# State products of two groups moved into the core visits before them, and one group cut into blocks of 64 tokens

## The chip, the core and the metric

The kernel runs on one core of a Trainium2 chip. The metric is the device time of one execution in microseconds. Before the change the median was 227.49 us over three runs (227.48 to 227.77). The kernel before was run again beside every experiment, on the same chip. A run more than 1.5% above the fastest of the same kernel counts as slow, and slow runs enter no comparison here.

The engines are written as in the profile: PE is TensorE (PEld its weight loads), DVE is VectorE, ACT is ScalarE, POOL is GpSimd and SP is SyncE. SP computes nothing here. It issues nearly all the loads, one after the other, so I call it the load queue. ACT issues the writes of the results.

## What must be computed

Linear attention with a decay per head comes first, then a SwiGLU feed-forward block (FFN) on its result. Cut to what matters:

```python
# q, k, v: (4 batches, 8 heads, 768 tokens, 64); lam: one decay per head
for each block of tokens:
    intra = (q k^T * mask of powers of lam) v       # scores, mask, product with v
    inter = (q * powers of lam) kv_state            # what came before the block
    out   = intra + inter
    kv_state = lam^block * kv_state + (k * powers of lam)^T v      # "state products"
x   = out as (3072, 512)
res = (silu(x @ w_gate) * (x @ w_val)) @ w_out      # 512 -> 1536 -> 512
```

The reference takes blocks of 64 tokens. A kernel is free to take others, as long as the decays are right.

## The kernel before

The work comes in 12 groups of 256 tokens. Two groups make a tile of 512 tokens, on which the FFN runs in 12 chunks of 128 columns. A chunk is four gate and four value products. A "step" is a chunk on a whole tile, and a "half step" is a chunk on one of its groups. The attention of a later group is dropped in between the steps of an earlier tile. TensorE then leaves its 128x128 FFN products for a burst of 64x64 products, and I call such a burst a visit.

A group below `NAT0` is taken in two blocks of 128 tokens. From `NAT0` on it is taken in four blocks of 64. This also decides how it is loaded:

```python
    NAT0 = 6
# ... cut ...
    def load_fp32(g, eng, src, what, h0=0, h1=H):
        # ... cut: the tile ...
        if g < NAT0:
            eng.dma_start(out=t[:, h0:h1], in_=gsrc(src, g, h0)[:, 0:h1 - h0])
            return
        # ... cut ...
        parts = [(0, 128, False)] if what == "v" else [(0, M, False), (M, M, True)]
        for s in range(2):
            for p0, n, rev in parts:
                eng.dma_start(out=t[p0:p0 + n, :, s * D:s * D + D], in_=...)
```

So a group in two blocks takes three loads (k, q, v). A group in four blocks takes ten (four for k, four for q, two for v), for the same bytes.

A group passes through these functions. `cast_scaled` makes bf16 of k (ACT) and q (DVE) and issues a transpose by DMA on the load queue. `v_scale` scales v on GpSimd. `scores` are the q k products, and their masks run on DVE. `upd_mm`, `upd_copy` and `state` are the state products on TensorE, their copies by ACT and the adding up on GpSimd. The core is the rest:

```python
    def guard(g):        # one column, copied by ACT: intra waits for it
        t = const.tile([128, 1], FP32, name="guard", tag="guard", bufs=2)
        nc.scalar.copy(out=t, in_=st[("op", g)][1][:, 511:512])
# ... cut ...
    def core_a(g):
        st[("op", g)] = [bank() for _ in range(2)]
        inter(g, True)
        guard(g)

    def core_b(g, fns=(nc.scalar.copy, nc.scalar.copy)):
        run_later(len(later))
        intra(g, False)
        evac(g, fns)
# ... cut ...
    def ahead(g):        # upd = upd_mm, upd_copy, state
        upd(g)
        scores(g)
```

A plan says after which step what comes. `s1a` and `s1b` are the half steps of tile 1 on its first and second group, and `s2` is the last of the first half steps of tile 2. The part concerned:

```python
    at(s1a[3], cast_scaled, 4)
    at(s1a[3], load_group, 5)
    for c in range(0, FC, 2):
        at(s1a[3], wo_piece, c, c + 2)
    # ... cut: scores and state products of 3 ...
    at(s1a[9], core_a, 3)
    at(s1a[10], core_b, 3, SPLIT)
    # ... cut ...
    at(s1b[3], cast_scaled, 5)
    at(s1b[3], load_group, 6)
    at(s1b[4], wo_cast)
    at(s1b[4], wo_cast)
    at(s1b[6], ahead, 4)
    # ... cut: three wo_cast, v_scale 5 ...
    at(s1b[9], core_a, 4)
    at(s1b[10], core_b, 4, SPLIT)
    at(s1b[10], wo_cast, ACTC)
    NH = 4
    s2 = [step(2, fc, 0, 2) for fc in range(NH)][-1]
    at(s2, load_group, 7, "kq")
    at(s2, ffn_out, 0, 0)
    at(s2, ahead, 5)
    at(s2, run_later, 3)
    at(s2, ffn_out, 0, 1)
    at(s2, core_a, 5)
    at(s2, ffn_out, 0, 2)
    at(s2, core_b, 5)
    at(s2, cast_scaled, 6)
    at(s2, load_group, 7, "v")
    at(s2, v_scale, 6, nc.gpsimd)
    at(s2, ffn_out, 0, 3)
```

`wo_piece` loads a sixth of w_out and `wo_cast` makes bf16 of it. `ffn_out(0, b)` is the output product of tile 0 (12 products over w_out), its copy by ACT and its write, issued by ACT. The order of the plan is also the order in which each engine meets its own instructions: nothing overtakes.

## Time and profile before

| | before |
|---|---|
| time, median of 3 | 227.49 us |
| span in the profile, mean clock | 226.7 us, 1.000 |
| busy: PE, DVE, ACT, POOL | 96%, 40%, 47%, 40% |
| first scores of 3 to the inter products of 6 | 48.44 to 99.67 us |

TensorE is the bound. This is the queue's own timeline before the change (start, duration, queue and source line, the kind of DMA, output and input, how many in a row):

```profile
49.03 1.18 SPq L100 DMA_DIRECT2D kraw<-in_k_dram  x1
50.25 0.93 SPq L100 DMA_DIRECT2D qraw<-in_q_dram  x1
51.22 1.03 SPq L100 DMA_DIRECT2D v<-in_v_dram  x1
...
78.28 3.08 SPq L107 DMA_DIRECT2D qraw<-in_q_dram  x4
83.43 2.01 SPq L256 DMA_TRANSPOSE qkt<-qk  x1
```

The first three lines are the loads of group 5, issued within 3.22 us. The fourth is q of group 7, issued in four pieces. The last is the transpose of group 6, whose scores TensorE reaches at about 91 us. It is issued some 8 us ahead.

### The profile page before, as it was taken

What the parts mean: (1) busy time and instruction counts of PE and PEld (TensorE: products, weight loads), DVE (VectorE), ACT (ScalarE), POOL (GpSimd) and SP (SyncE); (2) the same over time, 40 slices, a digit from 0 to 9 for tenths busy, and PEclk for the clock granted to TensorE, in tenths of its full rate; (3) what the DMA queues carried; (4) which work ended last, traced back from release to release, by engine and by line L of the source; (5) the groups of instructions that cost most, each with busy time, mean ns of one, the idle gap of its engine ahead of it and who ended that gap; (6) DMA issues with size and microseconds to landing.
All of it is one profiled execution on the core that took longest, in us unless ns stands there. A gap on an engine that the chain in (4) does not pass through costs nothing.

```text
span 226.7 us, 6032 instructions
## 1 busy us (share of the span) xinstructions
PE 218.6 (96%) x2492; PEld 121.5 (54%) x2504; DVE 91.0 (40%) x156; ACT 107.2 (47%) x212; POOL 90.1 (40%) x133
## 2 busy tenths in 40 slices
PE   8889979999999999999999999999999999999994
PEld 4565445887876465454544544544544444444442
DVE  2663446586763602733434362253242123222200
ACT  5878556655653263455454463453433433322321
POOL 6675636833492720968563092092160000000000
PEclk9999999999999999999999999999999999999999
DMA  6999999999998989197688848908101101101122
GB/s 200 344 345 328 371 314 326 260 174 343 402 208 195 230 214 264 46 236 186 164 185 220 210 109 210 247 8 142 49 1 46 49 0 46 46 3 46 46 93 93
DMA packets 88028, 39.70 MB, mean 175 GB/s; under 512 B 57666, under 2 KB 83522, under 8 KB 88002
## 3 DMA queue, kind: packets, MB, share of 16 engines
q1 hardware_dynamic: 83490, 32.58, 56.4%
q10 hardware_dynamic: 4512, 6.75, 8.3%
q8 instruction: 19, 0.31, 0.6%
q14 instruction: 7, 0.06, 0.1%
HBM read 28.31 MB, written 6.29 MB: 153 GB/s over the span
## 4 chain that ended last, share of the span: by engine, by line
PE 84%; DMA 7%; SPq 5%; POOL 2%; issue 1%; ACT 0%; DVE 0%; DVEq 0%
PE bank L552 27%; PE bank L519 25%; PE bank L534 24%; DMA qraw<-in_q_dram 4%; SPq L100 3%; DMA wraw<-in_moe_w_val_dram 3%; SPq L218 2%; PE bank L479 2%; PE bank L466 2%; PE bank L387 1%; PE bank L331 1%; PE bank L357 1%; PE bank L294 1%; POOL wv_sb L665 1%; POOL kvf L426 0%
## 5 line engine op out<-in xcount | busy, mean ns | idle before, releaser
L537 DVE TENSOR_TENSOR h<-sil,bank 128x512 bf16<-128x512 bf16 (+1 forms) x91 | 51.9, 576 | 108.3 <-PE bank L534 85.0
L519 PE MATMUL bank<-xt,wg_sb 128*128 128x512 bf16 (+1 forms) x364 | 77.2, 335 | 0.0
L534 PE MATMUL bank<-xt,wv_sb 128*128 128x512 bf16 (+1 forms) x364 | 77.0, 335 | 0.0
L523 ACT ACTIVATE sil<-bank 128x512 bf16<-128x512 f32 (+1 forms) x91 | 46.2, 511 | 43.2 <-PE bank L519 38.3
L552 PE MATMUL bank<-wo_sb,h 128*128 128x512 bf16 (+2 forms) x288 | 64.2, 370 | 0.8 <-issue 0.3
L534 PEld LDWEIGHTS <-wv_sb 128*128 128x128 bf16 x364 | 35.5, 98 | 27.0 <-POOL wv_sb L665 0.4
L519 PEld LDWEIGHTS <-wg_sb 128*128 128x128 bf16 x364 | 33.9, 98 | 26.3 <-DVE xt L491 0.5
L552 PEld LDWEIGHTS <-h 128*128 128x128 bf16 x300 | 28.6, 98 | 32.5
L554 ACT COPY osb<-bank 128x512 f32<-128x512 f32 (+1 forms) x24 | 14.0, 582 | 55.4 <-PE bank L552 55.4
L243 POOL TENSOR_TENSOR v_s<-v,dec 128x1024 bf16<-128x1024 f32 (+1 forms) x15 | 23.4, 1568 | 20.8 <-DMA v<-in_v_dram 10.8
L426 POOL TENSOR_TENSOR kvf<-kvs,ups 128x256 f32<-128x256 f32 x8 | 5.8, 728 | 34.6 <-ACT ups L409 32.0
L338 DVE TENSOR_TENSOR ssb<-bank,causal 128x512 bf16<-128x512 f32 x24 | 15.3, 684 | 4.5 <-PE bank L331 4.4
L491 ACT CAST xt<-bank 128x512 bf16<-128x512 f32 x20 | 12.2, 660 | 2.9 <-PE bank L479 2.4
L435 POOL CAST kvn<-kvf 64x256 bf16<-64x256 f32 x24 | 12.5, 520 | 1.5
L426 POOL TENSOR_TENSOR kvf<-kvf,ups 128x256 f32<-128x256 f32 x16 | 11.6, 726 | 0.6
L409 ACT COPY ups<-bank 128x256 f32<-128x256 f32 (+1 forms) x24 | 9.5, 449 | 2.4 <-PE bank L387 1.4
L263 ACT CAST qk<-kraw 128x1024 bf16<-128x1024 f32 x9 | 9.4, 1042 | 0.4 <-DMA kraw<-in_k_dram 0.4
L265 DVE TENSOR_TENSOR qk<-qraw,qdn 128x1024 bf16<-128x1024 f32 x6 | 8.2, 1372 | 2.6 <-DMA qraw<-in_q_dram 2.6
L362 DVE TENSOR_TENSOR ssb<-bank,causaln 128x512 bf16<-128x512 f32 x12 | 8.3, 688 | 1.2 <-PE bank L357 1.1
L237 POOL CAST wo_sb<-woraw 128x1024 bf16<-128x1024 f32 x5 | 5.1, 1042 | 6.3 <-DMA woraw<-in_moe_w_out_dram 6.3
L479 PE MATMUL bank<-ssb,v_s 64*64 64x128 bf16 (+1 forms) x384 | 6.7, 207 | 0.5 <-ACT guard L450 0.5
L479 PEld LDWEIGHTS <-v_s 64*64 64x64 bf16 x384 | 5.3, 105 | 2.0 <-issue 2.0
(66 smaller groups left out, 121.5 us busy)
## 6 DMA issues: line engine op xcount, KB each, us to landing
out_dram<-osb ACTq DMA_DIRECT2D x23, 256.0 KB, 2.9
v<-in_v_dram SPq DMA_DIRECT2D x18, 256.0 KB, 4.5
woraw<-in_moe_w_out_dram SPq DMA_DIRECT2D x6, 512.0 KB, 7.7
kraw<-in_k_dram SPq DMA_DIRECT2D x24, 128.0 KB, 3.8
qraw<-in_q_dram SPq DMA_DIRECT2D x24, 128.0 KB, 3.8
wraw<-in_moe_w_gate_dram SPq DMA_DIRECT2D x5, 512.0 KB, 7.5
wraw<-in_moe_w_val_dram SPq DMA_DIRECT2D x5, 512.0 KB, 6.5
kraw<-in_k_dram SPq DMA_DIRECT2D x4, 512.0 KB, 6.2
```

What stands on the lines that cost most here:

```text
L243: eng.tensor_tensor(out=st[("vs", g)][:, h0:h1], in0=st[("v", g)][:, h0:h1].rearrange("p h (s d) -> p h s d", s=2), in1=vfac(g, h0, h1), o ...
L338: nc.vector.tensor_tensor(out=ssb[:, h2, 2 * c:2 * c + 2].rearrange("p a s n -> p a (s n)"), in0=sp[(c, h2)].rearrange("p (a x) -> p a x", ...
L426: nc.gpsimd.tensor_tensor(out=o, in0=f, in1=u, op=ALU.add)
L435: nc.gpsimd.tensor_copy(out=o[64 - h2 * 64:128 - h2 * 64], in_=f[h2 * 64:h2 * 64 + 64])
L479: nc.tensor.matmul(op[r][h2 * 64:h2 * 64 + 64, cols(g, hp, s)], v_s[ps, 2 * hp + h2, s], ssb[ps, h2, hp * 2 + s] if g >= NAT0 else ssb[ps, ...
L491: fns[r](out=xt[:, g % 2, :, r].rearrange("p h (m s) -> p h s m", s=2) if g < NAT0 else xt[:, g % 2, :, :, r * M:r * M + M], in_=op[r].rea ...
L519: nc.tensor.matmul(gp[:, 0:N], wg_sb[:, mc, fs], xt[:, b0 // 2:b1 // 2, mc].rearrange("p g b n -> p g (b n)"), start=(mc == 0), stop=(mc = ...
L523: nc.scalar.activation(sil[:, 0:N], gp[:, 0:N], AF.Silu)
L534: nc.tensor.matmul(vp[:, 0:N], wv_sb[:, mc, fs], xt[:, b0 // 2:b1 // 2, mc].rearrange("p g b n -> p g (b n)"), start=(mc == 0), stop=(mc = ...
L537: nc.vector.tensor_tensor(out=h_sb[:, fc % FH, b0:b1].rearrange("p b n -> p (b n)"), in0=sil[:, 0:N], in1=vp[:, 0:N], op=ALU.mult)
L552: nc.tensor.matmul(ps, st[("h", t, fc // FH)][:, fc % FH, b], wo_sb[:, fc, c0:c1], start=(fc == 0), stop=(fc == FC - 1))
L554: fn(out=osb[:, c0:c1], in_=ps)
```

## The change

The intent has three parts. The state products of groups 4 and 5 move into the core visits of groups 3 and 4, between the inter and the intra products, where TensorE waits for the guard copy anyway. Group 5 becomes a group in four blocks of 64 tokens, which makes its scores, inter and intra products narrower. The order around it is fitted to this: one more half step before the first outputs, the cast of group 5 two half steps later, the last two pieces of w_out behind it, and the w_out casts spread over three engines.

```diff
-    NAT0 = 6
+    NAT0 = 5
@@
+    def core_upd(g, fns):
+        run_later(len(later))
+        core_a(g)
+        upd_mm(g + 1)
+        core_b(g, fns)
+        upd_copy(g + 1)
@@ the plan
     at(s1a[3], load_group, 5)
-    for c in range(0, FC, 2):
+    for c in range(0, 8, 2):
         at(s1a[3], wo_piece, c, c + 2)
@@
-    at(s1a[9], core_a, 3)
-    at(s1a[10], core_b, 3, SPLIT)
-    at(s1a[10], v_scale, 4, nc.gpsimd)
-    at(s1a[10], state, 3)
-    at(s1b[3], cast_scaled, 5)
-    at(s1b[3], load_group, 6)
-    at(s1b[4], wo_cast)
-    at(s1b[4], wo_cast)
-    at(s1b[6], ahead, 4)
+    at(s1a[8], v_scale, 4, nc.gpsimd)
+    at(s1a[8], state, 3)
+    at(s1a[10], core_upd, 3, SPLIT)
+    at(s1a[10], state, 4)
+    at(s1b[5], cast_scaled, 5)
+    at(s1b[5], wo_piece, 8, 10)
+    at(s1b[5], wo_piece, 10, 12)
+    at(s1b[5], load_group, 6)
+    at(s1b[5], v_scale, 5, nc.gpsimd)
+    at(s1b[6], scores, 4)
     at(s1b[6], run_later, 2)
-    at(s1b[6], wo_cast)
-    at(s1b[6], wo_cast)
+    at(s1b[7], wo_cast)
     at(s1b[8], wo_cast)
-    at(s1b[8], v_scale, 5, nc.gpsimd)
-    at(s1b[9], core_a, 4)
-    at(s1b[10], core_b, 4, SPLIT)
-    at(s1b[10], wo_cast, ACTC)
-    NH = 4
-    s2 = [step(2, fc, 0, 2) for fc in range(NH)][-1]
+    at(s1b[9], core_upd, 4, SPLIT)
+    at(s1b[9], wo_cast)
+    at(s1b[9], state, 5)
+    at(s1b[11], wo_cast, ACTC)
+    NH = 5
+    s2 = [step(2, fc, 0, 2) for fc in range(NH)]
+    at(s2[1], wo_cast, DVEC)
+    at(s2[3], wo_cast, ACTC)
+    s2 = s2[-1]
     at(s2, load_group, 7, "kq")
     at(s2, ffn_out, 0, 0)
-    at(s2, ahead, 5)
-    at(s2, run_later, 3)
+    at(s2, core_a, 5)
+    at(s2, scores, 5)
+    at(s2, run_later, 4)
     at(s2, ffn_out, 0, 1)
-    at(s2, core_a, 5)
+    at(s2, core_b, 5, SPLIT)
     at(s2, ffn_out, 0, 2)
-    at(s2, core_b, 5)
     at(s2, cast_scaled, 6)
```

## The prediction

> **What bounds the kernel now.** I read the busy shares first, then TensorE's waits, then the chain of waits. In the page, the busy line and TensorE's row over the 40 slices:
>
> ```profile
> PE 218.6 (96%) x2492; PEld 121.5 (54%) x2504; DVE 91.0 (40%) x156; ACT 107.2 (47%) x212; POOL 90.1 (40%) x133
> PE   8889979999999999999999999999999999999994
> ```
>
> TensorE is busy 96% of the span, without a hole from about 40 us on; no other engine reaches half. Busy alone is not proof, so I asked what TensorE (PE) waited for: eight rows, none over 1.2 us, of which the one of interest is:
>
> ```profile
> PE bank L479 <- ACT guard L450: 0.5, 2, 0.3
> ```
>
> (total us, times, longest). This is the wait of the intra products for the one-column ACT copy that follows the inter products, where nothing stands between the two. The chain of waits, in order of time, then gives the price of each piece of TensorE work (start, us, line, count):
>
> ```profile
> 51.45 0.34 PE bank L466 x8
> 51.79 0.54 PE bank L519 x4
> 52.33 0.44 PE bank L534 x4
> 52.77 0.57 PE bank L479 x32
> ...
> 60.49 0.38 PE bank L387 x32
> 60.87 0.45 PE bank L331 x32
> 61.32 0.54 PE bank L519 x4
> 61.86 0.44 PE bank L534 x4
> ...
> 64.04 0.60 PE bank L466 x16
> ...
> 76.85 0.57 PE bank L466 x16
> 77.42 2.69 PE bank L552 x12
> 80.12 0.57 PE bank L479 x32
> 80.69 0.16 issue
> ```
>
> ```profile
> 99.73 0.38 PE bank L466 x32
> 100.11 0.32 PE bank L387 x30
> 100.43 0.39 PE bank L357 x31
> 100.81 0.32 PE bank L479 x32
> ```
>
> A half step of the FFN is four gate and four value products of 256 columns, 0.44 + 0.44 us. After a visit of 64x64 products the first gate takes 0.54: leaving the small shape costs 0.10. Entering costs 0.10 too: the state products (L387) take 0.38 when they open a visit, and 0.28 where they follow the scores of group 3. L552 is the output product (12 of 0.216 us = 2.59; 2.69 after a visit). The second fence is a group in four blocks of 64 tokens; the others are groups in two blocks of 128. From there to the end the chain is TensorE, so time added or removed between 50 and 90 us moves the end one for one, as long as no wait appears.
>
> **What the Trainium skill says.** "TensorEngine Tiling (Array Packing)", Key Properties: "Changing tiling mode (not just tile) drains the TensorE". The trace agrees: 0.10 us in and 0.10 out. "TensorE: Matmul & The Clock Gate", Back-to-back issue gap, gives N/2.4 + 2.5 ns warm for an isolated gap. For 128 columns on a quarter of the array, 32 products are 8 per quarter, 8 x 55.8 = 0.45 us; the scores measure 0.45. For 64 columns it is 8 x 29.2 = 0.23; the trace has 0.28 to 0.39, so I use the trace. "DMA: Bandwidth & Descriptors", Specifications, asks 512 B for line rate. The change halves group 5's pieces to 256 B. The trace has 346 GB/s in 52 to 56 us (512 B and larger) and 275 in 66 to 67 (256 B). What bites more is issue time: group 5's three loads took 3.14 us on the queue's engine (1.18, 0.93, 1.03), group 6's ten took 8.95 (3.54, 2.68, 2.73).
>
> **The change part by part, on TensorE.** I list the visits after group 3's own state products, which stay.
>
> Before: core_a of 3, 0.34 + 0.10 exit; core_b of 3, 0.57 + 0.10; state products and scores of 4, 0.38 + 0.45 + 0.10. Sum 2.04. Core of 4: 0.60 + 0.10 and 0.57 + 0.10 = 1.37. Group 5 between outputs: state and scores 0.38 + 0.45 + 0.10 = 0.93; core_a 0.57 + 0.10 = 0.67; core_b 0.57 + 0.11 = 0.68 (0.16 issue, less 0.05 missing in the output piece after it). Total 5.69 us in eight visits.
>
> After: core of 3 with the state products of 4 in its middle: 0.34 + 0.28 + 0.47 + 0.10 = 1.19 (intra without an entry is 0.57 - 0.10). Scores of 4 alone: 0.10 + 0.45 + 0.10 = 0.65. Core of 4 with the state products of 5: 0.60 + 0.28 + 0.47 + 0.10 = 1.45. Group 5 in four blocks: inter 0.38, scores 0.33 (estimate between 0.29 where they follow the state products of group 6, and 0.39 above), exit 0.10 = 0.81; core_b 0.10 + 0.31 + 0.10 = 0.51. Total 4.61 us in five visits.
>
> Difference: 1.08 us. Of it 0.60 are three visits that go (3 x 0.20), and 0.48 are group 5's narrower products: 64 columns for 128 in scores (0.12), inter (0.19, though 32 instructions replace 16) and intra (0.16). Its state products stay 32 of 64 columns.
>
> Given back: one more half step pair in place of a full step, 16 x 109.4 ns against 8 x 216.2 = 0.02 us. The guard: bare, TensorE waited up to 0.3 us for it; in the new core visits 0.28 us of state products fill that gap, so about 0.03 us remains at each of two, say 0.06. Balance 1.08 - 0.08 = 1.00 us.
>
> Off TensorE: GpSimd gets four state adds of 0.73 us instead of two for group 5, and more casts (group 6: 7.4 us from 92.3 to 99.7, against 3.9 for group 5 at 74.9); of its five w_out casts three stay (one goes to ACT, which then has two, and one to DVE), so it gives away two of 1.04. It is at 40%, so this counts only through its deadlines. DVE saves two masks of about 0.65 us. Neither sets the end.
>
> **The rivals.** I follow each new deadline on the times of before, where the new order is by my sum some 0.1 us ahead at 64 us.
> First, late inputs of group 5. Loads start at 49.0, are issued until about 58.0, and v lands some 4.5 us after its issue (median in the page), at 61 to 62. v_scale is 1.92 us: ready at 63.9. The state products of 5 come, by my sum, at 64.5. Slack 0.6 us: the tightest place. If v lands 1.5 us later, TensorE loses about 1 us, and the whole gain is gone (227.5).
> Second, late w_out. The last two pieces are now issued behind the transpose of group 5, which is itself behind the first four pieces:
>
> ```profile
> 59.67 6.17 SPq L256 DMA_TRANSPOSE qkt<-qk  x1
> ```
>
> That transpose held the queue until the w_out traffic had drained (65.8 us). In the new order I expect the same end, about 66.3; then the pieces are issued by 67.3 and land at 70.5 and 71.5; DVE (0.84 us, twice its 128x512 cast of 0.42) and ACT (1.05 us) finish at 71.5 and 72.6. The first output starts at 71.6 and needs them at its 9th and 11th product, 73.3 and 73.7. Slack about 1.2 us. DVE and ACT sit behind these casts meanwhile; eight banks let TensorE run on. If they land 3 us late, the loss is about 2 us: 228.5.
> Third, late state of 5. GpSimd starts it at about 67.3, after the casts; the last block's state comes 5.4 us on (as for group 6, 92.3 to 97.7): 72.7, needed at 74.2. Slack 1.5 us; a miss of 1 us makes 227.0 to 227.5.
> Fourth, the gain is greater, if the 0.16 us issue gaps go too, or less if the drains merge with other waits: 226.2 to 226.9.
> Against all rivals of waiting speaks that the whole plan was moved with the loads (the cast of 5 two half steps later, w_out behind group 5, a fifth half step), which looks like a schedule fitted to these deadlines.
>
> **Range and chances.** 227.49 - 1.00 = 226.49. I give 60% to no new wait over 0.2 us, and some 35% to one of the three misses costing 0.3 to 1.2 us, so I move the centre to 226.6. The range runs from 226.0 (0.5 us more gain than summed) to 227.5 (the gain lost to one wait). A 2% change is 4.5 us: nothing in the sum reaches it; slower by that would take several stalls in a row, or a TensorE clock that falls. Faster 0.01, same 0.98, slower 0.01.
>
> **What would show it.** Right: TensorE's instructions on group 5 have 64-column forms (16 inter of 128 columns become 32 of 64); five visits in place of eight between 50 and 85 us in the chain; the fourth output product of tile 0 ends at about the same time as before (83.3), with one more half step already done. Wrong: a row of TensorE's waits naming v_s (L243), wo_sb (L237) or kvn (L435 or L437), of over 0.3 us; a guard wait well over 0.1 us at the two new cores; or group 5's inter in 64 columns costing as much as in 128. If the time falls by more than 1.5 us, the price of a visit is larger than I read it.

## More of the kernel before

The queue's own waits hold one line of interest (what waited, for what, total us, times, longest):

```profile
SPq L107 <- DMA out_dram<-osb: 1.8, 1, 1.8
```

A load waited 1.8 us for a write of the results. It stands far below the longest rows of that view, and nothing on TensorE waited for it.

## The result

The changed kernel is slower. Five runs took 233.70, 242.79, 232.79, 238.05 and 238.07 us, a median of 238.05, against 227.55 for five runs of the kernel before. Two of the five count as fast (233.70 and 232.79). Ratios here are the mean time of one kernel's fast runs over the mean of the other's fast runs of the same rounds, so they are not quite the ratio of the medians. This ratio is 1.0247, with a 95% interval of 1.0217 to 1.0278. The prediction was 226.6 us, with 1% for slower by over 2%.

The profile is of the run with 233.7 us (span 231.6 us, mean clock 0.992), and all that follows is about that run. From the page of the changed kernel, TensorE's row over the 40 slices of 5.8 us and the clock that was granted:

```profile
PE   8899999999996999699999999999999999999994
PEclk9999999999999999799999999999999999999999
```

Before, the row of TensorE was solid from 40 us on. Now it has two holes, at the 13th slice (69 to 75 us) and the 17th (93 to 98 us). In the second the clock dips too. TensorE's waits say what the holes are (what waited, for what, total us, times, longest):

```profile
PE bank L357 <- DMA qkt<-qk: 2.2, 1, 2.2
PE bank L552 <- ACT wo_sb L237: 1.7, 1, 1.7
PE bank L466 <- DVE ssb L338: 0.4, 1, 0.4
```

None of the three was among the waits before. The first is the scores of group 6, which wait for its transposed q and k. The second is the first output product, which waits for the last piece of w_out. The third is the core of group 4, which waits for the masks of its scores. I then measured TensorE's timeline between five landmarks, and set beside it what the prediction's own sums make of each stage (from its rounded pieces, so good to some 0.03 us):

| stage on TensorE, us | before | expected after | after | excess |
|---|---|---|---|---|
| first scores of 3 to scores of 4 | 11.98 | 12.06 | 12.24 | 0.18 |
| to the end of the core of 4 | 5.70 | 4.65 | 5.42 | 0.77 |
| to the first output | 4.46 | 6.21 | 6.13 | -0.08 |
| to the state products of 6 | 20.54 | 18.71 | 20.94 | 2.23 |
| to the inter products of 6 | 8.55 | 8.55 | 12.53 | 3.98 |
| sum | 51.23 | 50.18 | 57.26 | 7.08 |

The landmarks after are 47.27, 59.51, 64.93, 71.06, 92.00 and 104.53 us. From the inter products of group 6 on, the two kernels run alike. The whole span grew by less than 57.26 - 51.23 = 6.03 us, because this profile reached the first landmark 1.17 us earlier (47.27 against 48.44) with the same instructions: 6.03 - 1.17 = 4.86, and the spans differ by 4.9. Such starts vary from profile to profile (47.3 to 49.9 us in all of them), so I compare stretches rather than absolute times.

The last row is the largest. The chain of waits of the changed kernel around it (start, us, what):

```profile
88.93 5.69 DMA qkt<-qk
94.66 0.57 PE bank L357 x32
95.23 1.82 PE bank L519 x4
97.05 1.51 PE bank L534 x4
```

The transpose of group 6 is issued at 88.93 us. Its scores (L357) start when it has landed, at 94.66. The four gate products after them then take 1.82 us and the four value products 1.51, where the chain has 0.86 for four such products elsewhere, and 0.97 after a visit. Two windows show why (start and end, length, then the busy share and count of PE, PEld, DVE, ACT, POOL, then the clock, DMA share and GB/s):

```profile
93.00:94.00 1.00, 0.00 (x0) 0.00 (x0) 0.00 (x0) 1.00 (x3) 0.00 (x0) 1.00 1.16 305
...
97.00:98.00 1.00, 1.00 (x4) 0.30 (x2) 0.08 (x1) 0.60 (x1) 1.00 (x1) 0.50 0.00 0
```

TensorE stood idle in the first, and in the second it works at half the clock. The clock was at or near 0.50 from about 94.8 to 98.2 us, so for 3.4 us. The stage thus lost 2.49 us to the wait (92.00 to 95.16 where 0.67 was usual, so 3.16 - 0.67) and 1.82 + 1.51 - 0.97 - 0.86 = 1.50 us to the clock.

The Trainium skill's page "TensorE: Matmul & The Clock Gate", Part 1, has a table of two states of the clock, full and half, and says that half comes after an idle window of about 3.4 us. The trace agrees on the two states, and the half rate lasted 3.4 us. But the idle time that went before it here was 2.22 us, and an idle stretch of 1.75 us (73.7 to 75.5 us) left the clock at 1.00. The length of one idle stretch does not decide it, as two runs below show: in g2 an idle stretch of 2.35 us (114.19 to 116.54 us) left the clock at 1.00, and in e1 three stretches of 1.08, 1.05 and 0.92 us (between 99.71 and 103.65 us) went with 6.83 us at half clock.

Why was the transpose late? The load queue after the change answers that:

```profile
49.20 2.95 SPq L107 DMA_DIRECT2D kraw<-in_k_dram  x4
52.19 3.39 SPq L107 DMA_DIRECT2D qraw<-in_q_dram  x4
55.62 1.25 SPq L107 DMA_DIRECT2D v<-in_v_dram  x2
...
60.51 6.84 SPq L256 DMA_TRANSPOSE qkt<-qk  x1
67.39 1.09 SPq L232 DMA_DIRECT2D woraw<-in_moe_w_out_dram  x2
68.54 3.08 SPq L107 DMA_DIRECT2D kraw<-in_k_dram  x4
...
86.09 2.67 SPq L107 DMA_DIRECT2D qraw<-in_q_dram  x4
88.93 2.30 SPq L256 DMA_TRANSPOSE qkt<-qk  x1
```

The loads of group 5 now take from 49.20 to 56.87 us to issue, 7.67 us where three loads took 3.22. A piece of k or q (128 KB) costs the queue a median of 0.63 us, and a piece of v, of twice the bytes, 0.60. Everything behind shifts: the transpose of group 5 holds the queue until 67.35 us, the last pieces of w_out go out at 67.39 to 68.48, and k of group 6 at 68.54, where it was 65.89. By the transpose of group 6 the delay has doubled: 88.93 against 83.43, 5.5 us later. ACT's cast of k, its last input, was done at 84.66 us (83.40 before), so 4.3 us of this are the queue's. The queue's own waits tell where the delay grew:

```profile
SPq L107 <- DMA out_dram<-osb: 8.9, 5, 3.0
```

The loads now wait 8.9 us, five times, for writes of the results; before it was 1.8 us, once. A load has no use for a result. The two are tied by bookkeeping: in the compiled program, and in the semaphores of the trace, eight completion counters are dealt out in turn to all transfers of the load queue and of ACT's output queue, and a transfer may only start when the one that had its counter before has landed. After the change the loads of q of group 7 inherit their counters from the third and fourth output of tile 0. The third output is issued here (ACT's timeline):

```profile
83.17 0.34 ACTq L555 DMA_DIRECT2D out_dram<-osb  x1
```

It takes some 2.9 us to land, and at 86.09 the queue starts on q of group 7. The transpose of group 6 stands behind it in program order. The Trainium skill states the rule that makes this costly, in "DMA: Bandwidth & Descriptors", Anatomy of one DMA (a section on DMAs that GpSimd issues; here SP issues): "any semaphore wait happens on the issuing sequencer before dispatch". The trace agrees. The wait stood at the head of the queue, and the transpose, whose inputs were ready, could not pass it.

### The profile page after: what moved, and what is told of

It is laid out like the page before. It is cut to its first block, busy times and chain, and to the rows that moved or that the text cites. A ratio compares the mean times of both kernels' runs of the same rounds, so it can differ in the third digit from the quotient of the medians.

```text
span 231.6 us, 6107 instructions
## 1 busy us (share of the span) xinstructions
PE 220.9 (95%) x2528; PEld 123.1 (53%) x2528; DVE 90.8 (39%) x157; ACT 107.8 (47%) x213; POOL 89.9 (39%) x137
## 4 chain that ended last, share of the span: by engine, by line
PE 73%; DMA 13%; SPq 5%; DVE 3%; issue 2%; POOL 1%; ACT 1%; DVEq 0%
PE bank L552 25%; PE bank L519 21%; PE bank L534 20%; DMA qkt<-qk 4%; DMA qraw<-in_q_dram 4%; SPq L100 3%; DMA woraw<-in_moe_w_out_dram 3%; DMA wraw<-in_moe_w_val_dram 2%; SPq L218 2%; PE bank L479 2%; PE bank L466 2%; PE bank L357 1%; DVE ssb L338 1%; PE bank L387 1%; DVE qk L265 1%
## 5 line engine op out<-in xcount | busy, mean ns | idle before, releaser
L519 PE MATMUL bank<-xt,wg_sb 128*128 128x512 bf16 (+1 forms) x368 | 78.3, 336 | 0.0
L534 PE MATMUL bank<-xt,wv_sb 128*128 128x512 bf16 (+1 forms) x368 | 77.9, 335 | 0.0
L552 PE MATMUL bank<-wo_sb,h 128*128 128x512 bf16 (+2 forms) x300 | 65.8, 371 | 1.9 <-ACT wo_sb L237 1.7
L519 PEld LDWEIGHTS <-wg_sb 128*128 128x128 bf16 x368 | 34.7, 98 | 26.1 <-issue 0.5
L338 DVE TENSOR_TENSOR ssb<-bank,causal 128x512 bf16<-128x512 f32 x20 | 12.8, 684 | 1.8 <-PE bank L331 1.8
L426 POOL TENSOR_TENSOR kvf<-kvf,ups 128x256 f32<-128x256 f32 x18 | 13.1, 726 | 0.8
L491 ACT CAST xt<-bank 128x512 bf16<-128x512 f32 x19 | 11.4, 650 | 3.3 <-PE bank L479 2.8
L362 DVE TENSOR_TENSOR ssb<-bank,causaln 128x512 bf16<-128x512 f32 x14 | 9.5, 688 | 4.7 <-PE bank L357 4.5
L479 PE MATMUL bank<-ssb,v_s 64*64 64x64 bf16 (+1 forms) x384 | 6.5, 205 | 0.5 <-ACT guard L450 0.5
L226 POOL CAST wv_sb<-wraw 128x1024 bf16<-128x1024 f32 (+1 forms) x5 | 4.8, 956 | 3.3 <-DMA wraw<-in_moe_w_val_dram 3.2
```

What stands on the lines that cost most here:

```text
L338: nc.vector.tensor_tensor(out=ssb[:, h2, 2 * c:2 * c + 2].rearrange("p a s n -> p a (s n)"), in0=sp[(c, h2)].rearrange("p (a x) -> p a x", ...
L426: nc.gpsimd.tensor_tensor(out=o, in0=f, in1=u, op=ALU.add)
L479: nc.tensor.matmul(op[r][h2 * 64:h2 * 64 + 64, cols(g, hp, s)], v_s[ps, 2 * hp + h2, s], ssb[ps, h2, hp * 2 + s] if g >= NAT0 else ssb[ps, ...
L491: fns[r](out=xt[:, g % 2, :, r].rearrange("p h (m s) -> p h s m", s=2) if g < NAT0 else xt[:, g % 2, :, :, r * M:r * M + M], in_=op[r].rea ...
L519: nc.tensor.matmul(gp[:, 0:N], wg_sb[:, mc, fs], xt[:, b0 // 2:b1 // 2, mc].rearrange("p g b n -> p g (b n)"), start=(mc == 0), stop=(mc = ...
L534: nc.tensor.matmul(vp[:, 0:N], wv_sb[:, mc, fs], xt[:, b0 // 2:b1 // 2, mc].rearrange("p g b n -> p g (b n)"), start=(mc == 0), stop=(mc = ...
```

## The experiments

The theory after the first reading: the products of the change cost what was predicted, and the ten loads of group 5 make the load queue late, which brings the w_out wait and the transpose wait. Its main rival: the merged visits, or the form in four blocks, cost TensorE and its helpers more than read, and the queue is beside the point. Another: the short pieces of group 5's loads (256 bytes for 512) are slow as such, however many loads there are. In the expectations a letter A, alone or as A1 and A2, stands for readings in which the queue is the cause (its ties to the outputs, or the count of loads by itself), and B, C and D for what the text names. Twelve kernels were run. All outputs are right. A table first, then each one:

| run | built on | median us | ratio to before (95%) | waits on TensorE of over 0.3 us from the scores of 3 on, us |
|---|---|---|---|---|
| e1_transpose6_first | after | 238.79 | 1.047 (1.038 to 1.056) | state of 6 3.5, transpose of 8 2.0, w_out 0.6, masks 0.4 |
| e2_wo_early | after | 237.18 | 1.031 (1.028 to 1.035) | transpose of 6 3.9, of 5 0.4, masks 0.4 |
| e3_two_blocks | after | 229.41 | 1.008 (1.005 to 1.011) | masks 0.7 |
| e4_before_four_blocks | before | 239.41 | 1.053 (1.049 to 1.057) | states 5.3, transpose of 6 0.6 |
| f2_two_blocks_cast3 | after | 227.34 | 0.999 (0.996 to 1.002) | none over 0.3 |
| f3_out_gpsimd | after | 229.98 | 1.008 (1.004 to 1.012) | w_out 1.2, masks 0.4 |
| f5_two_blocks_ten_loads | after | 229.45 | 1.006 (1.002 to 1.010) | DVE 0.7, masks 0.7, v 0.6 |
| w1_upd_in_core | before | 227.50 | 0.999 (0.996 to 1.002) | none over 0.3 |
| g1_out_gpsimd_nh6 | after | 232.50 | 1.018 (1.013 to 1.024) | transpose of 8 1.9, w_out 0.7, masks 0.4 |
| g2_all_three_mended | after | 233.11 | 1.016 (1.010 to 1.023) | transpose of 8 2.4, w_out 1.5, state 1.2 |
| w1_again | before | 227.48 | 0.997 (0.993 to 1.001) | none over 0.3 |
| h1_t6_first_state_first | after | 235.72 | 1.032 (1.022 to 1.042) | w_out 1.8, v of 7 1.5, v of 4 0.8, masks 0.4 |

The medians are over all runs of a kernel, the ratios over fast runs. The kernel before had medians of 227.69, 228.08, 228.04 and 227.83 us beside them.

### e1: the transpose of 6 ahead of the loads of 7

```diff
 # on the changed kernel
-    at(s2, load_group, 7, "kq")
     at(s2, ffn_out, 0, 0)
@@
     at(s2, cast_scaled, 6)
+    at(s2, load_group, 7, "kq")
     at(s2, load_group, 7, "v")
```

> Edit: the changed kernel with one line moved: the loads of k and q of group 7 are issued after the cast and transpose of group 6, not before. Theory A (a late transpose of 6, because it stands in the load queue behind loads of group 7 that wait for output writes to land): the wait of the scores of 6 for the transpose (2.2 us in the profile) and the slow products after it (4 gate products 1.82 and 4 value products 1.51 us in place of 0.97 and 0.86, 1.5 us) go; the w_out waits (2.0 us) stay: about 233.2 - 3.7 = 229.5 us, with less spread between runs. Rival B (256-byte pieces make the transfers slow as such, whatever the order): 232 to 238 as before, the wait stays.

The transpose went out at 83.64 us and nothing waited for it, as expected. The time did not fall; it rose to 238.79. The loads of group 7 were now late instead. GpSimd's timeline and TensorE's waits, in turn:

```profile
97.70 1.91 POOL L243 TENSOR_TENSOR v_s<-v,dec 128x1024 bf16<-128x1024 f32 x1 [13.38 <-DMA v<-in_v_dram]
```

```profile
PE bank L466 <- POOL kvn L435: 2.4, 4, 1.1
```

GpSimd stood 13.38 us for v of group 7, with the state of group 6 behind it in its order, and the inter products of 6 waited 2.4 and 1.1 us for that state. Half clock followed. The queue is the scarce thing: what is let past in front makes another late.

### e2: all of w_out ahead of the transpose of 5, as before the change

```diff
 # on the changed kernel
-    for c in range(0, 8, 2):
+    for c in range(0, FC, 2):
         at(s1a[3], wo_piece, c, c + 2)
@@
-    at(s1b[5], wo_piece, 8, 10)
-    at(s1b[5], wo_piece, 10, 12)
```

> Edit: the changed kernel with all six w_out pieces issued before the transpose of group 5, as in the kernel before. Theory A: the waits for w_out (0.2 + 1.8 us) go, the outputs come 2 us earlier and with them the loads that wait for them, so the second wait (2.2 us) and the slow products stay: about 231.2. If the late outputs feed the second wait more than one for one, 228 to 230. Rival B: the transfers are full anyway and the transpose of 5 now comes late in place of w_out: 232 or more, with a wait of the inter or score products of 5 for their transpose.

The w_out wait is gone, and the stretch from the first output to the state products of 6 fell to 19.15 us, against 20.94. But the transpose of 5, which now follows six pieces of w_out, held the queue longer:

```profile
62.33 9.13 SPq L256 DMA_TRANSPOSE qkt<-qk  x1
```

The transpose of 6 followed at 88.50, TensorE waited 3.9 us for it and the half clock came again. The expectation of 231.2 was missed, and what rival B named came: over 232 us, with a wait of the inter products of 5 for their transpose (0.4 us). Both late w_out and the late transpose come from one queue, and mending one feeds the other.

### e3: group 5 in two blocks, all the rest of the change kept

```diff
 # on the changed kernel
-    NAT0 = 5
+    NAT0 = 6
```

> Edit: the changed kernel with group 5 in two blocks of 128 (three loads in place of ten), all else of the change kept. Theory A and B both: no long wait of TensorE; the visits saved are worth 0.6 us, of which 0.1 is given back: 226.9 to 227.3. Rival C (the state products inside the core visits, or the fifth half step, are what costs): over 230.

Both large waits are gone with three loads in place of ten, and the last two stages are 19.20 and 8.55 us. The time is 229.41, so the bulk of the loss is undone by this one number (it takes away the seven extra loads, the short pieces and the narrow products together). It still missed the expectation by 2 us. Its stage at the core of 4 is 5.95 us where 4.65 was the sum: the core waits twice for masks (0.33 and 0.39 us). The reason is on DVE. The cast of q of 5 now stands next to the four masks of group 4, and it took 1.75 us in this run against 1.22 in the changed kernel.

### e4: the kernel before with nothing but group 5 in four blocks

```diff
 # on the kernel before
-    NAT0 = 6
+    NAT0 = 5
```

> Edit: the kernel before with group 5 in four blocks of 64, nothing else of the change. Theory A: its narrower products save 0.48 us, but the ten loads push the w_out pieces and the transposes back, and the transpose of 6 now has to wait for the fourth output of tile 0 to land: 227.5 to 231, with a TensorE wait for a transpose. Rival C: no loss from the blocks, about 227.0. Rival B: the same slow runs as the changed kernel, 232 or more.

The time is 239.41: four blocks alone cost 12 us in the old order. TensorE's longest wait there:

```profile
PE bank L466 <- POOL kvn L437: 3.3, 2, 2.3
```

That line is for states of 4 and 5. On GpSimd the first w_out cast waited 9.08 us for its piece, because w_out stands behind the ten loads, and the state of 4 comes after it: 2.3 us of TensorE's wait. Most of the rest, 2.9 us, is for the state of 5 and does not come from the queue. Its adds and casts in four blocks start at 79.58 us, when ACT has copied the products, and run for some 5.4 us, while TensorE is at the inter products of 5 at 81.08. Half clock came twice, 3.41 us each time. The sign was as A expected; the number is the one that rival B named (232 or more), and this run does not part the two. The new order of the change was thus needed for four blocks, and did not suffice.

### f2: e3, with the cast of 5 back at its old place

```diff
 # on e3
-    at(s1b[5], cast_scaled, 5)
+    at(s1b[3], cast_scaled, 5)
```

> Edit: group 5 in two blocks with the rest of the change (as in e3), and the cast of group 5 moved back by two half steps to where the kernel before has it. Theory D (in e3 the scores of 4 and the core of 4 stand closer to the 1.22 us cast of q on VectorE, so the four masks are late and TensorE waits at the core of 4; its profile has 0.7 us of such waits, and the stretch from the scores to the end of the core is 1.2 us longer than the sum of its work): about 1.2 us less than e3, 228.2, no wait of the inter products for the masks. Rival: the time of e3 (229.4) comes from elsewhere, no gain.

The stage of the core of 4 fell from 5.95 to 4.85 us, by 1.10 where 1.2 was expected, and the mask waits are gone. With 227.34 the kernel is level with before. This explains the third row of the waits above: it is the cast's place on DVE. It needs no late queue, since e3 has three loads.

### f3: the four outputs of tile 0 issued by GpSimd

```diff
 # on the changed kernel
-            if last else ((0, DM, nc.scalar.copy, nc.scalar),)
+            if last else ((0, DM, nc.scalar.copy, nc.gpsimd if t == 0 else nc.scalar),)
```

> Edit: the changed kernel, with the four output writes of the first tile issued from GpSimd's queue, so that no load of groups 6 and 7 has to wait for one of them (in the changed kernel four loads reuse the completion semaphore of an output write, and the second piece of v of 6, and two loads of q of 7, were issued right when an output landed). Theory A1 (these waits make the load queue late): the transpose of 6 is issued at about 85 in place of 89, the 2.2 us wait and the 1.5 us of slow products go: 229.5. Theory A2 (the queue is late because it has ten more issues of 0.65 us each in a row): little change, 232 to 237.

This cuts the tie between loads and outputs and leaves the ten loads. The queue waited 1.7 us for writes, in place of 8.9, and the transpose of group 6 went out earlier:

```profile
84.30 2.67 SPq L256 DMA_TRANSPOSE qkt<-qk  x1
```

That is 4.6 us earlier than in the changed kernel, and nothing waited for it. The clock was 1.0 in all runs; one of the four still took 233.64 us, counts as slow and has no profile. The stretch from the scores of 3 to the inter products of 6 is 52.38 us, 4.88 of the 7.08 us of excess are gone, and the median is 229.98 for 229.5 expected. Late w_out (1.2 us) and the masks (0.4) stay. So in this order the coupling through the counters is what made the late queue cost a transpose wait and a half clock. The edit also takes four issues (0.34 to 0.41 us each) off ACT, which no run separates.

### f5: two blocks, but ten loads

```diff
 # on e3
-    at(s1a[3], load_group, 5)
+    for src, what, n in ((k, "kraw", 2), (q, "qraw", 2), (v, "v", 4)):
+        for h0 in range(0, H, n):
+            at(s1a[3], load_fp32, 5, nc.sync, src, what, h0, h0 + n)
```

> Edit: group 5 in two blocks (as in e3, 229.4 us), its loads cut by heads into ten in place of three; the pieces stay 512 bytes long. Theory A2 (number of issues): w_out, the loads of 6 and 7 and the transpose of 6 are as late as in the changed kernel, TensorE waits for w_out or the transpose: 232 or more. Theory B (256-byte pieces): as e3, 229 to 230.

Here the products are those of two blocks and the pieces 512 bytes long, but there are ten loads. k of group 6 goes out at 68.45 us, as in the changed kernel (68.54), and not as in e3 (65.93). So the queue's first delay comes from the count of loads and not from their short pieces. The time, 229.45, is the one that B expected, and A2's 232 or more did not come. The last w_out piece did land as late as in the changed kernel (74.40 us, there 74.35). It met no one, because TensorE itself took 25.90 us from the scores of 3 to the first output where e3 took 24.27 (it waited 0.6 us for v and 0.7 for DVE). The transpose of 6 was in time: it landed at 91.03 us, 1.8 us before its scores, and the queue had waited only 1.9 us for outputs. So late w_out needs no short pieces. The transpose wait did not come from ten loads alone, and whether the short pieces add to it is not shown. On DVE the cast of q of 5 took

```profile
59.74 2.77 DVE L265 TENSOR_TENSOR qk<-qraw,dec 128x1024 bf16<-128x1024 f32 x1
```

beside GpSimd's scaling of v (59.52 to 61.43), against 1.22 us alone. It is the third length of the same cast; no run isolates why.

### w1 and w1_again: the kernel before with nothing but the merged visits

```diff
 # on the kernel before (core_upd as in the change)
-    at(s1a[9], core_a, 3)
-    at(s1a[10], core_b, 3, SPLIT)
+    at(s1a[10], core_upd, 3, SPLIT)
+    at(s1a[10], state, 4)
@@
-    at(s1b[6], ahead, 4)
+    at(s1b[6], scores, 4)
@@
-    at(s1b[9], core_a, 4)
-    at(s1b[10], core_b, 4, SPLIT)
+    at(s1b[10], core_upd, 4, SPLIT)
+    at(s1b[10], state, 5)
@@
-    at(s2, ahead, 5)
-    at(s2, run_later, 3)
-    at(s2, ffn_out, 0, 1)
     at(s2, core_a, 5)
+    at(s2, scores, 5)
+    at(s2, run_later, 4)
+    at(s2, ffn_out, 0, 1)
+    at(s2, core_b, 5, SPLIT)
     at(s2, ffn_out, 0, 2)
-    at(s2, core_b, 5)
 # v_scale 4, v_scale 5 and state 3 some half steps earlier; loads, w_out, casts of q, NH as before
```

> Edit: the kernel before with only the merged visits: state products of 4 and 5 inside the cores of 3 and 4, scores of 5 beside the inter products of 5; group 5 in two blocks, four half steps, casts, loads and w_out where they were before, the core of 4 one half step later than in the change. If visits cost what the prediction says (0.2 us each, three gone) and no wait comes in: 227.0. Rival C (merged visits cost more than they save): 228 or more.

> The same kernel as w1_upd_in_core, in five rounds beside the kernel before: about 0.3 us below it (its stretch from the scores of 3 to the inter products of 6 was 50.86 against 51.23 us). The 95% interval will include or come near to 1.

227.50 and 227.48 us, with ratios of 0.9986 (0.9955 to 1.0017) and 0.9969 (0.9934 to 1.0005). The stretch took 50.86 us in w1's profile, 0.37 less than before, but 51.17 in that of w1_again, only 0.06 less, with no wait in TensorE's list in either. The merged visits are sound and gain between 0.1 and 0.3%, which the intervals do not separate from nothing. So the rival, as the cause of a loss of 5 us, is out.

### g1 and g2: the mends together

g1 takes f3 and adds a sixth half step before the outputs, so that w_out has more time. g2 adds the scores of 4 three half steps earlier, so that the masks are out of the cast's way.

```diff
 # g1, on f3
-    NH = 5
+    NH = 6
 # g2, on g1
-    at(s1b[6], scores, 4)
-    at(s1b[6], run_later, 2)
+    at(s1b[3], scores, 4)
+    at(s1b[3], run_later, 2)
```

> Edit: as f3 (output writes of the first tile from GpSimd's queue), and a sixth half step before the first output (0.875 us more time for the last w_out piece). The remaining w_out wait of f3's profile (1.2 us, stretch of the first output product 4.07 in place of 2.69 us) shrinks by 0.9 to some 0.3 us: 0.9 us less than f3, about 229.0 (f3's fast runs had 228.8 to 230.1). Rival (the w_out wait is hidden anyway, or moves on to another wait): no gain.

> Edit: as g1, and the scores of 4 three half steps earlier, so that their masks come before the cast of group 5 on VectorE. If the three causes are all there is, the stretch from the first score product of 3 to the inter products of 6 is the 51.23 us of before less the summed 1.0, some 50.3 to 50.6, and the time 226.7 to 227.2, faster than before by 0.2 to 0.4%. Rival (there is a fourth cost): 227.8 or more.

Both missed. In g1 the w_out wait fell from 1.2 to 0.7 us, but TensorE then waited 1.9 us for the transpose of group 8, which went out at 108.49 and held the queue for 2.93 us. In g2 the mask wait is gone as meant, and the state of a group (1.2), w_out (1.5) and the transpose of 8 (2.4) wait in its place. I expected sums of single mends; the runs gave new waits further on.

### h1: e1, with the state of 6 before the scaling of v of 7

```diff
 # on e1
-            at(sn[4], v_scale, 7, nc.gpsimd)
             at(sn[4], ahead, 6)
+            at(sn[4], v_scale, 7, nc.gpsimd)
```

> Edit: as e1 (transpose of 6 before the loads of 7), and on GpSimd the state of 6 before the scaling of v of 7. In e1 the transpose came in time, but v of 7, now the last of the late loads, landed at 97.7, GpSimd held the state of 6 behind it, TensorE waited 3.5 us for it at the inter products of 6, and the clock then read 0.5 for some 6 us. Theory A (the same lateness of the load queue, another victim): that wait goes, what stays is the w_out wait (0.6 us in e1), the masks (0.4), perhaps a short wait for the scaled v of 7: 229.5 to 232, against 236.6 to 240 of e1. Rival (e1's loss has another cause): 236 or more.

The wait for the state of 6, e1's longest, is gone, which shows that the order on GpSimd caused it. In its place TensorE waits 1.5 us for the scaled v of 7 and 1.8 us for w_out, where e1 had 0.6. 235.72 us is below e1 and lies between the two expectations. This profile also started late (scores of 3 at 49.89 us).

## Why the prediction was wrong

**The TensorE sum was nearly right.** The three visits that go should have saved 0.60 us, less 0.06 for the guard and 0.02 for the half step. In the runs without new waits the stretch is shorter than the 51.23 of before by 0.37 us (w1, 50.86), 0.31 (f2, 50.92) and 0.06 (w1_again, 51.17). Most of what w1 and f2 lack is the guard term, next; what w1_again lacks beyond it stays open. Group 5's narrower products can be read in the changed kernel itself: its inter products, its scores and the way out of them took 0.70 us (75.99 to 76.69); with the 0.10 of the way in, which lies before 75.99, that is the 0.81 of the sum. And in f3 the fourth stage is 20.07 us, of which 1.2 is the wait for w_out; the rest, 18.87, is close to the 18.71 of the sum. (The 0.45 and 0.23 us that the prediction works out from the skill's formula are estimates; its sum used the trace.)

**The guard term was mis-sized.** The sum had 0.03 us left of the guard at each merged core, and the intra products without an entry at 0.57 - 0.10 = 0.47. Neither held. In the core of group 2 before the change, which waits for the guard with nothing in between, the intra products started 0.66 us after the inter products (39.18 and 39.84 us) and the next gate 1.24 us after them. In f2's merged core of 3 the figures are 0.66 and 1.23 (51.11, 51.77 and 52.34 us). So the state products ride free in the guard's shadow, the guard still sets the start of the intra products, and these cost 0.57 as ever. The merged core of 3 is some 0.15 us longer than the sum. That makes most of the 0.18 in the first row, and twice 0.15 less the 0.06 allowed for is about the 0.2 us that w1 and f2 lack.

**The step that failed** is "I follow each new deadline on the times of before": the deadlines that it followed are those of v, w_out and the state of 5, and none of groups 6 and 7. The load queue is in order, and groups 6 and 7 stand behind the ten loads. The text itself gave the cost ("What bites more is issue time", 3.14 us for three loads against 8.95 for ten), but charged it to v of group 5 only. That one was the "tightest place", and it held: no wait for v of 5 is in TensorE's list. The transpose of 6 was never put on the list, and it cost 2.49 us for the wait and 1.50 for the clock, 3.98 of 7.08. f3 shows that this part goes when the counters are no longer shared with the outputs, and e3 that it goes with the ten loads and their short pieces.

**The second rival came true**, in mechanism and in size: "If they land 3 us late, the loss is about 2 us". DVE could start its cast at 72.01 us and ACT at 74.37, against landings of 70.5 and 71.5 in the text, and the stage lost 2.23. Two terms were too small. The pieces were issued until 68.48 and not until 67.3, and the second took 6 us or so in flight, not about 4. The page of before already had 7.7 us as the median from issue to landing of a w_out piece, so the shorter flight was my own choice. The chain shows the piece, its cast and the product that waited for it:

```profile
68.02 6.34 DMA woraw<-in_moe_w_out_dram
...
74.37 1.05 ACT wo_sb L237
...
75.47 0.59 PE bank L552 x2
```

The weight of this rival was far too low too.

**A cost that no part named** is the mask wait. The core of 4 has 0.77 us of excess, of which some 0.57 go with the masks: in f2, which has the same products there and no such wait, the stage takes 4.85 us in place of 5.42. The rest is the guard term above. The prediction saw that the cast of 5 comes two half steps later and did not ask what else DVE had there. Before, the cast and the four masks of group 4 were three half steps apart. Now the cast (59.15 to 60.37) runs into them, and they end at 63.42, where TensorE has reached the core at 62.88. f2 recovers 1.10 us of e3's stage by moving the cast alone.

**The argument against the rivals was no evidence.** It said that a plan moved together with its loads "looks like a schedule fitted to these deadlines". That made 60% for no new wait. The runs show the opposite: w_out early (e2), transpose early (e1), state early (h1), one half step more (g1) each open the next wait. With the ten loads TensorE waited for something late in every order that was tried with four blocks, and the order chose for what. The prediction also wrote that a loss of 2% "would take several stalls in a row, or a TensorE clock that falls". In the profiled run both came; it had given them 1%.

**What stays open.** Three of the five runs of the changed kernel took 238 to 243 us and have no profile. Their mean clocks (0.972, 0.993, 0.986) speak for more time at half clock in at least some of them, but with 0.993 one still took 238.05, so the clock alone does not cover it. Of the fast pair, the run of 232.79 had a mean clock of 1.000, so the half clock did not even come each time. Whether ten loads alone, without the shared counters and with TensorE on time, would still be late for the transpose is answered by f3 for this order only. Why the transpose of 5 holds the queue for 2 us in some kernels and 9 in others was not tested by itself, but the traces show a pattern: it let the queue go just before the last w_out piece issued ahead of it landed (67.35 and 67.52 us after the change, 65.84 and 65.97 before, 71.46 and 71.62 in e2, 67.25 and 67.44 in f5). An attempt to load both token halves in one transfer, to keep four blocks with fewer loads, did not build: the pattern has too many dimensions. No version beat the kernel before beyond the intervals. If one part is to be kept, it is w1.

## What to carry to other kernels

Count issues as well as bytes when a change splits a load: on an in-order queue each piece takes its time from everything behind it, so trace the deadlines of the next two groups and not only of the one that changed. Look through the waits of the queue itself for things a load has no business waiting for, such as output writes, since shared completion counters can turn a small delay into a long one. And where a single mend moves a wait instead of removing it, take the cause away (here ten loads to three) before ordering further.

## What the Trainium skill lacked or had wrong

- "DMA: Bandwidth & Descriptors", Issuing engines are not separate DMA queues, calls the sequencer's time to initiate a DMA "usually small relative to the DMA itself". Here a load of 128 KB took the queue a median of 0.63 us, against 3.4 us from issue to landing, and the ten loads of group 5 took it 7.67 us. What that alone cost is not shown: in two blocks the time was 229.45 us with ten loads (f5) and 229.41 with three (e3).
- The same page has no word on how long a DMA transpose holds its queue while earlier transfers are outstanding. In the changed kernel it was 1.6 to 2.3 us from 84 us on, but 6.84 us right behind four pieces of w_out, and 9.13 behind six (e2).
- No page that I read says that completion counters dealt out in turn tie loads to output writes on another queue. It cost 8.9 us of the load queue's time in the changed kernel, against 1.8 before, and issuing those outputs from GpSimd brought it to 1.7.
- "TensorE: Matmul & The Clock Gate", Part 1, puts the fall to half clock after an idle window of about 3.4 us. Here half clock followed a single idle stretch of 2.22 us in the profiled run of the changed kernel, and not one of 2.35 us in g2; in e1 it came with three stretches of 0.92 to 1.08 us.
